# Retention and two expert layers on one core: the steps of the w_in product by quarters tied in issue order on TensorE, the softmaxes on VectorE, one more buffer for the last output weight

## Chip, cores, metric

One NeuronCore of a Trainium2 chip runs the whole program. The metric is the device time of one execution in microseconds (us). Three executions of the kernel before took 999.73 to 1002.95 us, median 1002.52. The profiled execution took 998.94 us and its span, from the first to the last instruction, is 997.2 us.

## What is computed

A decaying linear attention over 4 batches, 8 heads, 768 positions (3072 tokens of 512 values), then a gated layer (RMS norm, gate and value of 1536, silu times value, back to 512), then a second layer on which this change works:

```python
def _moe2_ref(x, w_in, w_out, g_ln):       # x: 3072 x 512
    h = x @ w_in                           # 512 -> 1024
    e = np.exp(h - np.max(h, -1, keepdims=True))
    sm = e / (np.sum(e, -1, keepdims=True) + 1e-09)
    solu = h * sm
    mu = np.mean(solu, -1, keepdims=True)
    var = np.mean((solu - mu) ** 2, -1, keepdims=True)
    ln = (solu - mu) / np.sqrt(var + 1e-06) * g_ln
    return ln @ w_out                      # 1024 -> 512
```

## The kernel before

The tokens go through in six passes of 512 (n = 0 to 5). All products are of float32 accuracy: each factor is split into a high and a low part, and a product is three matmuls, high by high, high by low, low by high. `split` (L99) does that, the high part by a cast on ScalarE (L100), the low part by a subtraction on VectorE or GpSimd (L101).

A pass has two stages. In the first (`bc_block`, in pass 5 `seven_block`, L913) the gate and value products go to the PSUM banks GB and VB (in pass 5 also SB and YB), and the output product, `cmm`, adds up over twelve weights in the banks X0 to X3; the result is the pass's x, transposed. Pieces of the next pass's attention run between (L119, banks SB and YB), with its masks on VectorE (L262).

In the second stage (`de_quarters`, L1086, in passes 2 to 5) x times w_in is made by seven products of quarter matrices in place of eight, for two blocks of 128 rows each: 14 steps, `p1` to `p7`, each of six matmuls of 128x512 in `mul` (L1136). Step names below carry the row block: p4(0) is p4 for block 0. A step's bank is emptied by a copy on ScalarE (`keep`, L1145) or by an addition on VectorE (`add`, L1149), and then serves a later step: GB takes p1(0), p6(0), p7(0), p4(0) in turn, VB takes p1(1), p6(1), p7(1), p4(1). The second operands of p5 (T1) lie in two of the four buffers "w4" in which weights are loaded; those of p6 and p7 lie in xnh and xnl, which hold the normed input of the first stage and are filled for the next pass when p6 and p7 are through: xnl by four subtractions on GpSimd, in pass 4 by three (L101).

The result has four tiles of 128 rows by 1024 columns, t = 0 to 3. `soft(t)` makes the softmax part: two maxima (L986) and their join (L987) on VectorE, two exponentials on ScalarE (L989), two products with sums on VectorE (L994), and the subtraction of the mean (L999), columns 0 to 511 on VectorE, 512 to 1023 on GpSimd. `t_tr(t)` transposes the two halves into X0 and X1 by four matmuls each (L1010) and splits each half for the output product, `e_mm(t)`: 24 matmuls into GB, X2 or X3 (L771 to L773), the first twelve with the first half. p4(0) is the last part of tile 2, p3(0) of tile 0, p4(1) of tile 3, p3(1) of tile 1, and the tiles go through in the order 2, 0, 3, 1.

No engine's order is the order of the text. A scheduler puts the instructions of each engine in order at compile time, by its own estimate of when each can start; `tc.issue_after(i)` ties the instructions of a block behind i on i's engine, and `high_priority` brings forward. Before the change the steps p1 to p7 are tied to each other hardly at all, and of the four softmaxes only soft(0) is, behind the drains that came before it.

In pass 5 the twelve output weights (512 KB each) come through two buffers "wo": `out(i)` (L919) does `cmm` for weight i and issues the load of weight i + 2, which needs the buffer that weight i has just left. Weight 11 is thus loaded once `cmm` 9 is done. The loads of xnh and xnl for the second stage (L1078) are tied behind the last of these on the SP queue.

## Time and profile before

| what | value |
|---|---|
| median of three runs (lowest, highest) | 1002.52 us (999.73, 1002.95) |
| the profiled execution's own time | 998.94 us |
| its span | 997.2 us |
| TensorE busy in the span | 966.0 us, 97% |
| VectorE, ScalarE, GpSimd busy | 506.4, 422.5, 455.6 us |
| second stage of passes 2, 3, 4, 5 begins near | 478, 640, 800, 942 us |
| last matmul begins | 993.5 us |

A group's idle time is that of its engine just before the group's instructions, and what ended it is inferred from semaphores. A matmul's time in the trace contains its run through the array: six matmuls of 128x512 in a row are issued every 0.227 us, though each shows about 0.39.

### The profile page before, as it was taken

The numbers are of one execution on the slowest core, as the hardware profiler recorded it, in microseconds if no ns is written. First come the engines' busy times: TensorE is split into PE (matmuls) and PEld (weight loads), VectorE is DVE, ScalarE is ACT, GpSimd is POOL, SyncE is SP. The second block draws the span as 40 slices with busy tenths as digits, with TensorE's granted clock in tenths as the row PEclk, the third lists the DMA queues.
The fourth block names the chain that finished last, engine by engine and source line by source line (L and its number), as shares of the span: only waits on it lengthen the run. The fifth ranks groups of instructions, "written<-read, shape, count | busy, mean of one in ns | idle before, by whom it ended". The sixth has DMA issues, their size and how long they took to land.

```text
span 997.2 us, 16099 instructions
## 1 busy us (share of the span) xinstructions
PE 966.0 (97%) x5868; PEld 800.6 (80%) x5868; DVE 506.4 (51%) x992; ACT 422.5 (42%) x824; POOL 455.6 (46%) x537
## 2 busy tenths in 40 slices
PE   8989999999999999999989999989999999999988
PEld 7867887888888888888768888868888878999866
DVE  5787784652464644333582223565223367343572
ACT  4767665581353443223463222355322356212343
POOL 6976782870242794444373244456133446000023
PEclk9899999999999999999999999999999999999999
DMA  9799999987422127997642899832699855697401
GB/s 357 248 332 400 348 314 375 344 276 233 143 64 88 49 74 248 309 307 252 228 138 94 286 333 305 298 107 99 205 332 316 312 175 170 199 313 247 170 1 43
DMA packets 94991, 227.65 MB, mean 228 GB/s; under 512 B 10816, under 2 KB 36800, under 8 KB 93888
## 3 DMA queue, kind: packets, MB, share of 16 engines
q1 hardware_dynamic: 86128, 201.44, 59.6%
q10 hardware_dynamic: 8784, 25.17, 6.5%
q8 instruction: 47, 0.77, 0.3%
q14 instruction: 32, 0.26, 0.1%
HBM read 184.63 MB, written 41.94 MB: 227 GB/s over the span
## 4 chain that ended last, share of the span: by engine, by line
PE 84%; DVE 6%; DMA 5%; ACT 2%; POOL 2%; issue 1%; SPq 0%; ACTq 0%; POOLq 0%
PE X L771 10%; PE X L773 10%; PE X L772 10%; PE GB L773 6%; PE GB L771 6%; PE GB L772 6%; PE VB L771 5%; PE VB L773 5%; PE VB L772 5%; PE SB L119 3%; PE GB L1136 2%; PE X L1136 2%; PE VB L883 2%; PE YB L883 2%; PE VB L1136 2%; DMA x<-in_wpk 2%
## 5 line engine op out<-in xcount | busy, mean ns | idle before, releaser
L790 DVE TENSOR_TENSOR f<-VB,f 128x512 f32<-128x512 f32 x60 | 41.4, 690 | 147.6 <-PE VB L773 126.0
L771 PE MATMUL X<-r,wo 128*128 128x512 f32 x264 | 102.1, 394 | 1.2 <-DMA wo<-scr 1.2
L772 PE MATMUL X<-r,wo 128*128 128x512 f32 x264 | 103.2, 391 | 0.0
L773 PE MATMUL X<-r,wo 128*128 128x512 f32 x264 | 103.0, 390 | 0.0
L819 ACT ACTIVATE f<-GB 128x512 f32<-128x512 f32 x60 | 35.8, 596 | 146.3 <-PE GB L773 143.8
L100 ACT CAST r<-f 128x512 fp32r<-128x512 f32 x72 | 44.6, 619 | 117.9 <-DVE f L790 99.5
L672 POOL TENSOR_TENSOR st<-st,x 128x512 int32<-128x512 int32 x52 | 70.0, 1349 | 47.7 <-DVE st L671 11.2
L771 PE MATMUL GB<-xnh,w 128*128 128x512 f32 (+1 forms) x220 | 85.9, 390 | 1.8 <-ACT xnh L100 1.0
L771 PE MATMUL VB<-xnh,w 128*128 128x512 f32 (+1 forms) x220 | 85.8, 390 | 0.0
L773 PE MATMUL VB<-xnh,w 128*128 128x512 f32 (+1 forms) x220 | 85.2, 387 | 0.3 <-POOL w L101 0.3
L772 PE MATMUL GB<-xnl,w 128*128 128x512 f32 (+1 forms) x220 | 85.0, 386 | 0.3 <-DVE xnl L101 0.2
L773 PE MATMUL GB<-xnh,w 128*128 128x512 f32 (+1 forms) x220 | 84.9, 386 | 0.3 <-DVE w L101 0.3
L772 PE MATMUL VB<-xnl,w 128*128 128x512 f32 (+1 forms) x220 | 85.0, 386 | 0.0
L567 POOL TENSOR_TENSOR x<-x 128x512 f32<-128x512 f32 x24 | 31.3, 1306 | 105.0 <-DMA x<-scr 66.9
L101 DVE TENSOR_TENSOR r<-f,r 128x512 fp32r<-128x512 f32 x72 | 59.8, 831 | 32.5 <-ACT r L100 31.7
L101 POOL TENSOR_TENSOR r<-st,r 128x512 fp32r<-128x512 f32 x8 | 10.3, 1293 | 115.7 <-ACT r L100 113.9
L771 PEld LDWEIGHTS X<-r,wo 128*128 128x128 f32 x264 | 49.6, 188 | 11.9 <-issue 1.6
L773 PEld LDWEIGHTS X<-r,wo 128*128 128x128 f32 x264 | 49.6, 188 | 10.4
L772 PEld LDWEIGHTS X<-r,wo 128*128 128x128 f32 x264 | 49.6, 188 | 10.1 <-issue 0.2
L771 PE MATMUL X<-w2oh,r 128*128 128x512 f32 (+1 forms) x144 | 56.7, 394 | 0.1
L773 PE MATMUL X<-w2oh,r 128*128 128x512 f32 (+1 forms) x144 | 56.4, 392 | 0.0
L772 PE MATMUL X<-w2ol,r 128*128 128x512 f32 (+1 forms) x144 | 55.7, 387 | 0.0
(445 smaller groups left out, 2474.5 us busy)
## 6 DMA issues: line engine op xcount, KB each, us to landing
w<-scr SPq DMA_DIRECT2D x96, 512.0 KB, 5.1
wo<-scr SPq DMA_DIRECT2D x60, 512.0 KB, 5.2
x<-in_wpk SPq DMA_DIRECT2D x36, 512.0 KB, 6.5
x<-scr SPq DMA_DIRECT2D x24, 512.0 KB, 6.1
sscr<-x SPq DMA_DIRECT2D x24, 512.0 KB, 7.8
scr<-CV ACTq DMA_DIRECT2D x18, 512.0 KB, 6.3
rv<-in_kv SPq DMA_DIRECT2D x24, 256.0 KB, 4.6
scr<-w ACTq DMA_DIRECT2D x12, 512.0 KB, 5.9
```

Of the source, the lines that this page charges most:

```text
L100: h = nc.scalar.copy(hi, src)
L101: (lo_eng or nc.vector).tensor_tensor(out=lo, in0=src, in1=hi.bitcast(F32), op=ALU.subtract)
L119: return lambda: nc.tensor.matmul(out, lhsT=lhsT, rhs=rhs, start=start, stop=stop)
L567: nc.gpsimd.tensor_tensor(out=w[:, 0, :], in0=w[:, 0, :], in1=w[:, 1, :], op=ALU.add)
L672: nc.gpsimd.tensor_tensor(out=ti, in0=ti, in1=lo, op=ALU.add)
L771: nc.tensor.matmul(ps, lhsT=lh, rhs=rh, start=start, stop=False)
L772: nc.tensor.matmul(ps, lhsT=lh, rhs=rl, start=False, stop=False)
L773: return nc.tensor.matmul(ps, lhsT=ll, rhs=rh, start=False, stop=stop)
L790: recent["dve"] = nc.vector.tensor_tensor(out=a, in0=GV[1], in1=silu[:, 0, :], op=ALU.mult)
L819: recent["act"] = nc.scalar.activation(s[:, 0, :], GV[0], AF.Silu)
L883: nc.tensor.matmul(ps, lhsT=x, rhs=y[:, k, :], start=start and k + i == 0, stop=k == 1 and i == 2, skip_group_check=True)
L1136: nc.tensor.matmul(bank, lhsT=x[:, k, ts_], rhs=y[:, k, :], start=start and k + i == 0, stop=k == 1 and i == 2, skip_group_check=True)
```

## The change

Four edits:

- `mul`: each of its matmuls is tied behind the one before it, so that TensorE issues the steps in the order of the text: p1(0), p1(1), p2(0), p6(0), p5(0), p7(0), p6(1), p4(0), p3(0), p7(1), p5(1), p2(1), p4(1), then the transposes of tile 2, then p3(1).
- p3(1) is tied behind the transposes of tile 2 on TensorE, and its addition behind the low parts of tile 2 on VectorE (`recent["t"]`, `recent["lo"]`, noted in `t_tr`).
- On VectorE soft(3) is tied behind the mean subtraction of soft(0) and the low parts of tile 2; soft(1) behind the mean subtraction of soft(3).
- In pass 5 weight 11 gets a buffer of the pool "x2" and its load is issued in `out(8)`.

```diff
@@ seven_block, out(i)
                 cmm(base + i, i)
-                if i + 2 < NM:
+                if i + 2 < NM - 1:
                     w_load(base + i + 2, 2)
+                if i + 3 == NM - 1:
+                    t = wsp[base + NM - 1, 2] = wt("x2", [P, 2, 512], F32R, 4)
+                    nc.sync.dma_start(t.bitcast(F32), scr[NM - 1][2])
@@ t_tr
-            run([lambda j=j: nc.tensor.transpose(bank[:, j * P:j * P + P], u[:, b, j * P:j * P + P], ident)
+            recent["t"] = run([lambda j=j: nc.tensor.transpose(bank[:, j * P:j * P + P], u[:, b, j * P:j * P + P], ident)
                  for j in range(4)])
             hi, lo = r2(), r2()
-            split(hi, lo, bank)
+            nc.scalar.copy(hi, bank)
+            recent["lo"] = nc.vector.tensor_tensor(out=lo, in0=bank, in1=hi.bitcast(F32), op=ALU.subtract)
@@ de_quarters, mul
-                    nc.tensor.matmul(bank, lhsT=x[:, k, ts_], rhs=y[:, k, :], start=start and k + i == 0,
-                                     stop=k == 1 and i == 2, skip_group_check=True)
+                    with tc.issue_after(last["mm"].ins) if "mm" in last else nullcontext():
+                        last["mm"] = nc.tensor.matmul(bank, lhsT=x[:, k, ts_], rhs=y[:, k, :],
+                                                      start=start and k + i == 0, stop=k == 1 and i == 2,
+                                                      skip_group_check=True)
@@ de_quarters, after p4(1)
-        soft(n, 3, (VB, u[3][:, 1, :]), halves(e2()), u[3], False)
-        p3(1, X3)
-        soft(n, 1, (u[1][:, 0, :], u[1][:, 1, :]), halves(e2()), u[1], True)
+        with tc.issue_after(recent["sub"].ins), tc.issue_after(recent["lo"].ins):
+            soft(n, 3, (VB, u[3][:, 1, :]), halves(e2()), u[3], False)
+        last["mm"] = recent["t"]
+        with tc.issue_after(recent["lo"].ins):
+            p3(1, X3)
+        with tc.issue_after(recent["sub"].ins):
+            soft(n, 1, (u[1][:, 0, :], u[1][:, 1, :]), halves(e2()), u[1], True)
```

The instructions are the same in number and kind; what moves is their order. On TensorE in the second stage of pass 2 (f4_572 is tile 2 after its softmax, VB takes p4(1), X3 takes p3(1)), before, right behind the end of p4(1) and 16 attention matmuls:

```order
L1010 MATMUL X0_68<-ident_182,f4_572_4605 128x128 x4
L1136 MATMUL X3_71<-w2ih_1728,r2_566_4561 128x512
L1136 MATMUL X3_71<-w2il_1729,r2_566_4561 128x512
L1136 MATMUL X3_71<-w2ih_1728,r2_567_4562 128x512
L1136 MATMUL X3_71<-w2ih_1728,r2_566_4561 128x512
L1136 MATMUL X3_71<-w2il_1729,r2_566_4561 128x512
L1136 MATMUL X3_71<-w2ih_1728,r2_567_4562 128x512
L1010 MATMUL X1_69<-ident_182,f4_572_4605 128x128 x4
```

And now, right behind p4(1):

```order
L1013 MATMUL X0_68<-ident_182,f4_572_4605 128x128 x4
L1013 MATMUL X1_69<-ident_182,f4_572_4605 128x128 x4
L1141 MATMUL X3_71<-w2ih_1728,r2_566_4561 128x512
L1141 MATMUL X3_71<-w2il_1729,r2_566_4561 128x512
L1141 MATMUL X3_71<-w2ih_1728,r2_567_4562 128x512
L1141 MATMUL X3_71<-w2ih_1728,r2_566_4561 128x512
L1141 MATMUL X3_71<-w2il_1729,r2_566_4561 128x512
L1141 MATMUL X3_71<-w2ih_1728,r2_567_4562 128x512
```

The second half's transposes come ahead of p3(1); in passes 3 and 5 they moved in the same way, and in pass 4 six matmuls of pass 5's first product stand between the two halves. Further up, p4(0) was the 11th of the steps and is now the 8th, and p5(1) was the 9th in pass 4 and is now the 11th.

On VectorE in the second stage of pass 5 (sm_1104 is tile 0, sm_1110 tile 3, sm_1112 tile 1; X0 holds the first half of tile 2's transposes), before:

```order
L986 TENSOR_REDUCE sm_1104_8868<-f4_1096_8779 128x1 x2
L986 TENSOR_REDUCE sm_1110_8918<-VB_67 128x1
L986 TENSOR_REDUCE sm_1112_8938<-f4_1097_8787 128x1
L986 TENSOR_REDUCE sm_1110_8918<-x2_1101_8851 128x1
L101 TENSOR_TENSOR r2_1106_8892<-X0_68,r2_1105_8891 128x512
L987 TENSOR_REDUCE sm_1104_8868<-sm_1104_8868 128x1
L1149 TENSOR_TENSOR f4_1097_8787<-X3_71,f4_1097_8787 128x512
```

And now:

```order
L989 TENSOR_REDUCE sm_1104_8868<-f4_1096_8779 128x1 x2
L1155 TENSOR_TENSOR f4_1097_8787<-X2_70,f4_1097_8787 128x512
L990 TENSOR_REDUCE sm_1104_8868<-sm_1104_8868 128x1
L997 SCALAR_TENSOR_TENSOR f4_1096_8779,sm_1104_8868<-f4_1096_8779,st_1102_8866 128x512
L997 SCALAR_TENSOR_TENSOR f4_1096_8779,sm_1104_8868<-f4_1096_8779,st_1103_8867 128x512
L1022 TENSOR_SCALAR sm_1104_8868<-sm_1104_8868 128x1
L1017 TENSOR_TENSOR r2_1106_8892<-X0_68,r2_1105_8891 128x512
```

Tile 0 is carried through ahead of the maxima of tiles 3 and 1, which stand behind the low parts of tile 2.

On the SP queue at the end of pass 5's first stage (wo and x2_1073 take output weights, xnh and xnl the operands of p6 and p7), before:

```order
L700 DMA wo_1059_8483<-scr8_2_113 128x1024
L872 DMA A_1060_8505<-scr11_0_120 128x2x256
L700 DMA wo_1062_8524<-scr9_2_116 128x1024
L872 DMA A_1063_8545<-scr11_1_121 128x2x256
L1082 DMA w4_1079_8702<-t2scr0_135 128x1024
L1082 DMA w4_1080_8703<-t2scr0_135 128x1024
L700 DMA wo_1072_8631<-scr10_2_119 128x1024
L700 DMA wo_1078_8700<-scr11_2_122 128x1024
L1078 DMA xnh_78<-t2scr1_136 128x2048
L1078 DMA xnl_79<-t2scr2_137 128x2048
```

And now:

```order
L925 DMA x2_1073_8633<-scr11_2_122 128x1024
L700 DMA wo_1059_8483<-scr8_2_113 128x1024
L872 DMA A_1060_8505<-scr11_0_120 128x2x256
L700 DMA wo_1062_8524<-scr9_2_116 128x1024
L872 DMA A_1063_8545<-scr11_1_121 128x2x256
L1086 DMA w4_1079_8702<-t2scr0_135 128x1024
L1086 DMA w4_1080_8703<-t2scr0_135 128x1024
L700 DMA wo_1072_8631<-scr10_2_119 128x1024
L1082 DMA xnl_79<-t2scr2_137 128x2048
L1082 DMA xnh_78<-t2scr1_136 128x2048
```

The load of weight 11 moved ahead of those of weights 8, 9 and 10, and xnl's load ahead of xnh's.

## Rows read from the trace of the kernel before

**Rows 1.** The page, part 1: busy time, share of the span, instructions.

```profile
PE 966.0 (97%) x5868; PEld 800.6 (80%) x5868; DVE 506.4 (51%) x992; ACT 422.5 (42%) x824; POOL 455.6 (46%) x537
```

**Rows 2.** By stretch: us; busy PE, PEld, DVE, ACT, POOL; PEclk, DMA share, GB/s.

```profile
540.00:640.00 100.00, 100.00 (x561) 82.20 (x560) 33.18 (x58) 27.63 (x54) 38.82 (x44) 1.00 0.89 300
...
478.00:540.00 62.00, 56.81 (x382) 45.79 (x381) 36.80 (x91) 31.67 (x67) 33.74 (x50) 1.00 0.40 131
640.00:700.00 60.00, 55.81 (x390) 44.92 (x389) 36.79 (x89) 30.78 (x65) 34.18 (x51) 1.00 0.39 123
798.00:835.00 37.00, 33.69 (x172) 27.85 (x171) 29.16 (x70) 22.69 (x49) 24.16 (x23) 1.00 0.41 141
935.00:994.00 59.00, 52.85 (x262) 42.54 (x260) 31.07 (x78) 25.01 (x54) 15.75 (x26) 1.00 0.16 61
```

**Rows 3.** TensorE's waits: us in total, times, longest us.

```profile
PE X L1010 <- DVE f L999: 4.9, 4, 1.7
PE SB L119 <- DVE A L262: 4.1, 2, 2.0
PE VB L1136 <- ACT x L1145: 2.7, 3, 0.9
PE YB L119 <- ACT sq L321: 2.5, 2, 1.2
PE GB L773 <- DVE sm L987: 1.9, 2, 1.0
...
PE X L771 <- DMA wo<-scr: 1.2, 1, 1.2
...
PE SB L883 <- POOL xnl L101: 0.9, 1, 0.9
...
PE X L1010 <- DVE r L101: 0.4, 1, 0.4
```

**Rows 4.** Timeline of TensorE, pass 5: start, us, what, [idle before <-releaser].

```profile
946.22 1.52 PE L1136 MATMUL GB<-xnh,r 128*128 128x512 f32 x6
...
958.23 0.39 PE L1136 MATMUL X<-w2ih,r 128*128 128x512 f32 x1
959.52 0.50 PE L1136 MATMUL VB<-w2ih,x 128*128 128x512 f32 x1 [0.90 <-ACT x L1145]
...
966.04 0.50 PE L773 MATMUL GB<-w2oh,r 128*128 128x512 f32 x1 [1.00 <-DVE sm L987]
...
973.01 1.26 PE L1010 MATMUL X<-ident,f 128*128 128x128 f32 x8 [1.69 <-DVE f L999]
```

**Rows 5.** Timeline of VectorE, pass 5: tile 2 from its maximum to its mean subtraction.

```profile
957.30 0.69 DVE L986 TENSOR_REDUCE sm<-GB 128x1 f32<-128x512 f32 x1 [3.36 <-PE GB L1136]
...
961.33 0.49 DVE L999 TENSOR_SCALAR f<-f,sm 128x512 f32<-128x512 f32 x1
```

**Rows 6.** Timeline of GpSimd, pass 5.

```profile
961.49 1.77 POOL L999 TENSOR_SCALAR f<-f,sm 128x512 f32<-128x512 f32 x1
```

**Rows 7.** Timeline of GpSimd, pass 2.

```profile
493.95 5.03 POOL L101 TENSOR_TENSOR xnl<-xT,xnh 128x512 fp32r<-128x512 f32 x4 [2.07 <-PE VB L1136]
...
501.68 1.57 POOL L999 TENSOR_SCALAR f<-f,sm 128x512 f32<-128x512 f32 x1
...
515.32 1.81 POOL L999 TENSOR_SCALAR f<-f,sm 128x512 f32<-128x512 f32 x1
```

**Rows 8.** Timeline of VectorE, pass 2.

```profile
515.69 1.09 DVE L994 SCALAR_TENSOR_TENSOR f<-f,x 128x512 f32<-128x512 f32 x1
```

**Rows 9.** Timeline of TensorE, pass 2.

```profile
497.05 0.39 PE L1136 MATMUL X<-w2ih,r 128*128 128x512 f32 x1
```

**Rows 10.** Timeline of TensorE, pass 4.

```profile
815.36 0.39 PE L1136 MATMUL X<-w2ih,r 128*128 128x512 f32 x1
```

**Rows 11.** Timeline of GpSimd, pass 4.

```profile
812.93 3.77 POOL L101 TENSOR_TENSOR xnl<-xT,xnh 128x512 fp32r<-128x512 f32 x3 [2.82 <-PE VB L1136]
```

**Rows 12.** DMA issues of 805 to 822 us: KB each, median us to landing.

```profile
w<-scr SPq DMA_DIRECT2D x1, 256.0 KB, 3.5
```

More of the change, by code (lines that the diff above doesn't have):

```diff
@@ L1129, in de_quarters @@
         T2, T3 = ((t[:, 0:2], t[:, 2:4]) for t in (xnh, xnl))
-        sl = [base]
+        sl, last = [base], {}
         def mul(bank, t, A, B, start=False):
@@ L1154, in de_quarters @@
         (GB, VB), (X0, X1, X2, X3) = GV, XB
-        u, last = {}, {}
+        u = {}
         def p1(t, Z):
```

## The prediction

> **What bounds the kernel now.** I read the page's first part, then the stretches, then TensorE's waits, then the timelines of the second stages. TensorE is busy 966.0 of 997.2 us [rows 1], so all that an order of issue can win is its 31 us of idle time, wherever that is not filling or draining. The stretches say where it is not: in the body of pass 3, from 540 to 640 us, TensorE has no idle time at all, while the four windows around the second stages, 218 us in all, have 5.2, 4.2, 3.3 and 6.2 us of it (62.00 less 56.81, and so on), 18.8 us together, at a granted clock of 1.00 throughout [rows 2]. The list of waits names them: eight kinds, 16 waits, 18.6 us [rows 3]. None of them is a lack of work in general. Each is one matmul at the head of TensorE's queue whose operand is late, while work for which nothing was missing stood behind it: p4(1) behind a copy of VB by ScalarE (2.7 us), transposes behind a mean subtraction (4.9 us), attention behind squares and masks that queued among four softmaxes (2.5 and 4.1 us).
>
> A wait costs a little more than its idle time. The last matmul of p3(0) was issued at 958.23 and the next, at a pace of 0.227 us (six in 1.36 us: the first of p6(0) starts at 946.22 and its six end 1.52 us later, 0.16 of it the last one's run through the array), was due at 958.46. It came at 959.52, 1.06 us late for an idle time of 0.90 [rows 4]. So 0.16 us more for each, 2.6 us for the 16: the waits cost 21.2 us. That is the ceiling of the gain.
>
> **The change part by part.** Nothing is added or removed but the place of instructions, so each part is costed by the waits that it ends and those that it makes.
>
> *Weight 11's buffer.* TensorE stood 1.2 us for this load [rows 3]. Its new place on the SP queue is ahead of the loads of weights 8 to 10, all of which landed in time before, and the buffer was last used for block 4. Gain 1.2 + 0.16 = 1.35 us, between 1.0 (if the operands for p6 become late next) and 1.35. What now follows it on the queue, xnl and xnh, is first used 4.1 us and 6.8 us into the second stage (xnh by p6(0), the 4th step, xnl by p7(0), the 6th, at 1.36 us a step) and is issued earlier than before; I take nothing for it.
>
> *Steps in order, pass 5.* p4(0) is the 8th step in place of the 11th, so tile 2's softmax begins 3 x 1.36 = 4.1 us earlier. Before, it took 4.5 us from its maximum at 957.30 to the end of the mean subtraction at 961.82 [rows 5], and GpSimd's half another 1.4 us, to 963.26 [rows 6]. Three steps back from 957.30 is 953.2, so the halves are done at 957.7 and 959.2. The 13 steps, which begin at 942.14, end at 942.14 + 13 x 1.36 = 959.8. Both transposes of tile 2 find their operand ready: that wait and the one for the copy of VB are gone, the copy now having two steps (2.7 us) between p7(1) and p4(1). Next is the output product of tile 2. Its third matmul needs the low part of the first half, and is due at 959.8 + 1.3 (eight transposes, as at 973.01) + 1.36 (p3(1)) + 0.45 = 962.9, where it came at 966.04 before [rows 4]. VectorE has seven operations of 128x512 between 957.7 and the end of that low part (two additions, two maxima, two products, the low part), at 0.69 us each [rows 5] 4.8 us, which gives 962.5; if the products must wait a us for ScalarE's exponentials, 963.5. I take a wait of 0.5 us (0 to 1.2) and so 963.4: 2.6 us gained. The later waits of the pass, 1.7 and 0.4 us with 0.16 each, 2.4 us, were those for tiles 0 and 3, whose mean subtractions now come one after the other with an output product of 5.4 us (24 x 0.227) between; I take both as gone. With the weight, pass 5 gains 6.4 us (4 to 7.2).
>
> *Passes 2 and 3.* Waits before: 0.9 for the copy, 1.2 for squares, 2.0 for masks in each (a third or a half of the totals in [rows 3]), and 1.0 for a subtraction in pass 2: 5.2 and 4.2 us of idle time [rows 2], 5.8 and 4.7 with the 0.16. What is late next is GpSimd. Its half of tile 2's subtraction stands behind the four subtractions for the next pass's xnl, which start when p7(1) has read xnl and take 5.03 us, from 493.95 to 498.98 [rows 7]. p7(1) is the 10th step before and now, so that does not move. The half then ends at 498.98 + 0.2 + 1.57 = 500.8. Before, the transposes that need it stood behind p3(1) and later waits hid it; now they come straight after the first half's. Twelve steps are done 0.227 us after 497.05 [rows 9], the thirteenth at 498.6, the first half's transposes at 499.3: a new wait of 1.5 us, 1.7 with its restart, in each of the passes, with p3(1) and all else behind it. GpSimd may be slower still: the same half took 1.81 us at 515.32, beside a VectorE product that took 1.09 in place of 0.69 [rows 7, 8]; that adds 0.25. I take 1.8 us for each. The masks and squares no longer queue among softmaxes: the attention products stand twelve output matmuls later. Gain 4.0 and 2.9 us (2 to 5.8, 1 to 4.7).
>
> [...]
>
> *Pass 4.* Waits before 3.3 us [rows 2], 3.8 with restarts. Twelve steps end at 815.58 [rows 10], the thirteenth at 816.9, the first transposes at 817.5. Six matmuls of pass 5 come next, whose weights wait for a buffer of T1, free when p5(1) is done, two steps later than before: 814.2, and 3.5 us to land [rows 12], 817.7. Then the second half's transposes: GpSimd is through xnl at 816.70 [rows 11], and 0.2 + 1.81 later at 818.7, when TensorE is there at 818.4. Two waits of 0.2 and 0.3 with restarts, 0.8 us. Gain 3.0 us (1.5 to 3.8).
>
> **Sum.** 6.4 + 4.0 + 2.9 + 3.0 = 16.3 us. Against the profiled execution's own 998.94 that is 982.6. The three runs stand 0.8 to 4.0 us above that execution, their median 3.6; in such runs I expect 983.4 to 986.6, and put down **984.8**. All upper ends (7.2 + 5.8 + 4.7 + 3.8 = 21.5, with the profiled execution's own level) give 977.4, all lower ends (8.5, at the median's level) 994.
>
> **Rivals.**
>
> *GpSimd and the chain behind it hold more.* In passes 2 to 4 the low parts of tile 2, and by the new ties soft(3), p3(1)'s addition and soft(1), stand behind transposes that stand behind GpSimd. If each half takes 1.5 us longer than I summed, as it would with one more GpSimd operation of 1.3 to 1.8 us ahead of it, the waits come again at tile 3's transposes and at the masks. For it: those spans on GpSimd are the least sure. Passes 2 to 4 then gain some 3 us of 9.9, the sum is 9.4, the time 991.7. Chance 0.15.
>
> *The passes' bodies take it back.* The transfers are busy 0.89 of the body at 540 to 640 us [rows 2]; if they set the pace there, TensorE arriving earlier only waits later for weights. Against it: TensorE waits for no weight there now, the second stages leave transfers at 0.40, and each load is set off by TensorE's own progress. Only pass 5 then gains: 998.94 - 6.4, with the runs' level 995. With pass 5 at its lower end it is inside 0.3% (some 3 us, what a measurement of this kernel can tell from no change). Chance 0.08.
>
> *Slower: the softmaxes one by one.* Before, the maxima, exponentials and products of tiles 0, 3 and 1 overlapped on VectorE and ScalarE; tied, tile 3 starts only behind tile 2's second low part, and tile 1 behind tile 3, each a chain of 4.5 us [rows 5] and GpSimd's 1.8. In pass 5 nothing else is left for TensorE. By the same count tile 3's second half is done some 1 us before its transposes are due. To lose 3 us in all, the four passes would have to lose the 16.3 us and 3 more, 4.8 us each, so each chain must run about 6 us longer than its rows: then 1004 to 1008. Against it: between the tiles TensorE has 5.4 us of output product each. Chance 0.05.
>
> *It does next to nothing*, because the scheduler had the order nearly so. Against it: p4(0) moves by three steps in all four passes. What would be left is the weight's 1.35 us. Chance 0.04.
>
> **Numbers.** The forecast has 0.68. Faster by over 0.3%: it, the first rival and most of the second, 0.89; within 0.3%: 0.06; slower: 0.05. The range for 8 in 10 takes in the forecast's own span and the first rival's time: 978 to 994.
>
> **What would show it.** Right: no wait for the weight near 938 us; no wait of VB's p4(1) on ScalarE; about 1.5 us of wait at the second transposes in passes 2 and 3, ended by GpSimd's subtraction and none such in pass 5; TensorE's idle time in the four windows down from 18.8 to some 5 us; the bodies without waits. Wrong: a wait of over 3 us at any transposes, waits for weights in a body, or waits at tile 3's or tile 1's transposes in pass 5.

## The result, and the profile after

| | before | after |
|---|---|---|
| median of the runs | 1002.38 us (four, 999.73 to 1002.95) | 989.88 us (four, 989.03 to 991.99) |
| ratio, with 95% interval | | 0.9884 (0.986 to 0.9908) |
| the profiled execution, its span | 998.94, 997.2 us | 989.03, 987.2 us |

A second set on another occasion gave 990.05 us against 1003.2, ratio 0.988 (0.9854 to 0.9905). The change makes the kernel 1.2% faster, 12.5 us between the medians. Faster was forecast, and the time lies within the range, but 5 us above the forecast of 984.8 and nearer to the first rival's 991.7.

From one start of p1(0) to the next in TensorE's timeline, and from the last to the last matmul, the profiled executions compare as follows. This leaves out the start of the program up to pass 2's second stage, which no edit touches and which took 478.6 to 484.5 us in the executions profiled for this study. The kernel before's profiled execution is one of its faster ones (998.94 us at a granted clock of 0.997; 43 others took 998.06 to 1006.67 at 0.988 to 0.995), which may be why the table gives 10.4 us and the medians 12.5.

| stretch, us | before | after | difference | forecast |
|---|---|---|---|---|
| pass 2's second stage, pass 3's first | 160.83 | 158.85 | -1.98 | -4.0 |
| pass 3's second stage, pass 4's first | 159.79 | 158.20 | -1.59 | -2.9 |
| pass 4's second stage, pass 5's first | 142.89 | 141.30 | -1.59 | -3.0 - 1.35 |
| pass 5's second stage | 51.38 | 46.14 | -5.24 | -5.05 |
| sum | 514.89 | 504.49 | -10.40 | -16.3 |

Pass 5 came as summed. Passes 2 to 4 gave 3.7 us of 9.9, the weight's part left out.

In the rows of after, t_tr's and soft's lines stand 3 further than before and `mul` at L1141: L997 is soft's product, L999 the join of its sums, L1002 the mean subtraction, L1013 the transposes, L1017 the low part, L1151 `keep`, L1155 `add`. The page's part 1 (as [rows 1]):

```profile
PE 966.5 (98%) x5868; PEld 803.6 (81%) x5868; DVE 511.7 (52%) x992; ACT 422.0 (43%) x824; POOL 455.3 (46%) x537
```

By stretch (columns as in [rows 2]), a body first, then the four second stages:

```profile
540.00:636.00 96.00, 96.00 (x543) 78.92 (x542) 31.83 (x55) 24.45 (x47) 39.47 (x45) 1.00 0.90 305
478.00:540.00 62.00, 59.87 (x391) 48.70 (x390) 39.83 (x89) 33.10 (x71) 32.75 (x49) 0.97 0.40 135
637.00:697.00 60.00, 56.84 (x369) 46.23 (x367) 37.30 (x87) 32.01 (x69) 34.36 (x51) 1.00 0.41 133
796.00:833.00 37.00, 34.07 (x171) 27.76 (x170) 30.42 (x70) 21.74 (x46) 22.88 (x21) 1.00 0.37 129
930.00:984.00 54.00, 53.03 (x270) 44.03 (x268) 32.44 (x81) 26.53 (x57) 14.49 (x26) 1.00 0.13 53
```

The body has no idle time, as before, so the transfers took nothing back. The second stages still have 2.1, 3.2, 2.9 and 1.0 us, 9.2 where 18.8 were and 5 forecast, and in the first the granted clock is 0.97. TensorE's waits (as [rows 3]):

```profile
PE X L1013 <- POOL f L1002: 4.8, 3, 2.1
PE GB L773 <- DVE r L1017: 2.0, 2, 1.7
...
PE X L1141 <- DVE r L101: 1.1, 2, 0.5
...
PE SB L119 <- DVE A L262: 0.9, 1, 0.9
```

Of the eight kinds before, six are gone, those for VB's copy, the squares, the weight and VectorE's mean subtraction among them; of the masks one of two is left. The third matmul of tile 2's output product still waits for the low part, 1.71 us in pass 4 and 0.26 in pass 5. Before, it waited 0.88 and 1.00 there, under the name of the join L987 in [rows 3, 4]: the low part ended at 965.98 us, 0.06 ahead of the matmul, and the join in the same moment as the matmul began. What is new: the second transposes wait for GpSimd's half of tile 2 (2.13, 2.12 and 0.54 us in passes 2, 3 and 4, none in pass 5), and p5(0) for S1's low part (0.54 in passes 4 and 5). Pass 2 in the timelines, GpSimd first, then VectorE (between its rows the mean of tile 2 is made), then TensorE:

```profile
494.37 5.67 POOL L101 TENSOR_TENSOR xnl<-xT,xnh 128x512 fp32r<-128x512 f32 x4 [1.62 <-PE VB L1141]
500.00 0.19 POOL L1024 TENSOR_TENSOR sm<-sm 128x1 f32<-128x1 f32 x1
500.17 1.57 POOL L1002 TENSOR_SCALAR f<-f,sm 128x512 f32<-128x512 f32 x1
```

```profile
494.43 0.68 DVE L997 SCALAR_TENSOR_TENSOR f<-GB,x 128x512 f32<-128x512 f32 x1
...
495.03 1.18 DVE L997 SCALAR_TENSOR_TENSOR f<-f,x 128x512 f32<-128x512 f32 x1
...
496.27 1.11 DVE L999 TENSOR_TENSOR sm<-sm 128x1 f32<-128x1 f32 x1
...
497.61 1.29 DVE L1002 TENSOR_SCALAR f<-f,sm 128x512 f32<-128x512 f32 x1
498.82 0.68 DVE L1155 TENSOR_TENSOR x<-X,x 128x512 f32<-128x512 f32 x1
```

```profile
499.06 0.60 PE L1013 MATMUL X<-ident,f 128*128 128x128 f32 x4
501.79 0.65 PE L1013 MATMUL X<-ident,f 128*128 128x128 f32 x4 [2.13 <-POOL f L1002]
```

The four subtractions for xnl took 5.67 us where they had taken 5.03 [rows 7]. Beside them three VectorE operations were drawn out: a product of two SBUF tiles 1.18 us, an addition of two columns 1.11, a mean subtraction 1.29. In pass 5, with no GpSimd operation on two tiles beside them, the same three take 0.69, 0.15 and 0.49. Operations that read PSUM (the product from GB, the addition from X) kept 0.68, and so did the maxima. The softmax of tile 2, three steps earlier than before, has moved onto the subtractions, and each holds up the other. In pass 4 GpSimd's quarter subtractions for pass 5 (L437) meet tile 0's products in the same way:

```profile
816.79 2.98 POOL L437 TENSOR_TENSOR xT<-xT 128x512 f32<-128x512 f32 x2
```

```profile
817.36 1.27 DVE L997 SCALAR_TENSOR_TENSOR f<-f,st 128x512 f32<-128x512 f32 x1 [0.94 <-ACT st L992]
...
818.56 1.76 DVE L997 SCALAR_TENSOR_TENSOR f<-f,st 128x512 f32<-128x512 f32 x1
...
820.38 0.67 DVE L1017 TENSOR_TENSOR r<-X,r 128x512 fp32r<-128x512 f32 x1
```

```profile
821.11 0.49 PE L773 MATMUL GB<-w2oh,r 128*128 128x512 f32 x1 [1.71 <-DVE r L1017]
```

And behind the wait of 2.13 us TensorE ran at half clock for a while (0.51 granted, in the first of these windows), as it did not behind that of 2.12 us in pass 3 (windows, columns as above):

```profile
502.70:506.10 3.40, 3.40 (x9) 2.61 (x9) 3.36 (x11) 3.33 (x10) 1.43 (x3) 0.51 0.00 0
661.50:664.90 3.40, 3.27 (x15) 2.37 (x14) 3.35 (x11) 3.33 (x10) 1.40 (x3) 1.00 0.00 0
```

At 0.51 the matmuls come every 0.427 us in place of 0.227; eight of them cost 1.6 us.

### The profile page after: what moved, and what is told of

It reads as the page before. It is cut to its first block, busy times and chain, and to the rows that moved or that the text cites. A ratio compares the mean times of both kernels' runs of the same rounds, so it can differ in the third digit from the quotient of the medians.

```text
span 987.2 us, 16094 instructions
## 1 busy us (share of the span) xinstructions
PE 966.5 (98%) x5868; PEld 803.6 (81%) x5868; DVE 511.7 (52%) x992; ACT 422.0 (43%) x824; POOL 455.3 (46%) x537
## 4 chain that ended last, share of the span: by engine, by line
PE 85%; DVE 5%; POOL 3%; DMA 2%; ACT 2%; issue 1%; SPq 0%; ACTq 0%; POOLq 0%; DVEq 0%
PE X L771 11%; PE X L772 10%; PE X L773 10%; PE GB L773 6%; PE GB L771 6%; PE GB L772 6%; PE VB L771 6%; PE VB L772 5%; PE VB L773 5%; PE SB L119 3%; PE YB L119 2%; PE VB L883 2%; PE YB L883 2%; PE GB L1141 2%; PE X L1141 2%; PE X L1013 2%
## 5 line engine op out<-in xcount | busy, mean ns | idle before, releaser
L772 PE MATMUL X<-r,wo 128*128 128x512 f32 x260 | 101.9, 392 | 0.0
L773 PE MATMUL X<-r,wo 128*128 128x512 f32 x260 | 101.4, 390 | 0.0
L771 PE MATMUL X<-r,wo 128*128 128x512 f32 x260 | 99.7, 394 | 0.0
L773 PEld LDWEIGHTS X<-r,wo 128*128 128x128 f32 x260 | 48.8, 188 | 10.2
L771 PEld LDWEIGHTS X<-r,wo 128*128 128x128 f32 x260 | 48.8, 188 | 10.2 <-ACT r L100 0.2
L772 PEld LDWEIGHTS X<-r,wo 128*128 128x128 f32 x260 | 48.8, 188 | 10.0 <-issue 0.2
```

The lines of the kernel that those rows point to most:

```text
L771: nc.tensor.matmul(ps, lhsT=lh, rhs=rh, start=start, stop=False)
L772: nc.tensor.matmul(ps, lhsT=lh, rhs=rl, start=False, stop=False)
L773: return nc.tensor.matmul(ps, lhsT=ll, rhs=rh, start=False, stop=stop)
```

## Experiments

Two theories of what was missing in passes 2 to 4. **Exclusion**: VectorE's products of SBUF tiles, additions and mean subtractions, with all operands in SBUF, and a running GpSimd operation hold each other up (in pass 2 a product of 0.69 us took 1.18, the four subtractions 5.67 for 5.03), and the change put such pairs side by side. **Queue**: GpSimd's half is late by its place in GpSimd's queue alone, the low part by its place in VectorE's, and the long durations have another cause. All runs below are told by the four stretches of the table above and their sum (after: 504.49).

**All of xnl behind tile 2's half.** `recent["g2"]` is GpSimd's subtraction in soft(2); in pass 4 the second and third of three are tied in the same way.

```diff
-    def xn_split_t(k):
-        with tc.issue_after(recent["hi"].ins):
+    def xn_split_t(k, n):
+        with tc.issue_after(recent["hi"].ins), tc.issue_after(recent["g2"].ins) if n > 2 and k >= 0 else nullcontext():
             split(xnh[:, k, :], xnl[:, k, :], xT[:, k, :], nc.gpsimd)
...
```

> The changed kernel with the subtractions for the next pass's xnl (four in passes 2 and 3, the second and third in pass 4) tied on GpSimd behind tile 2's half of the mean subtraction. Theory of exclusion (a VectorE operation whose operands all lie in SBUF and a running GpSimd operation hold each other up): with nothing on GpSimd beside it, tile 2's softmax in pass 2 goes back to 0.69 us for the second product (1.18 in the changed kernel), 0.15 for the join of the sums (1.11) and 0.49 for the mean subtraction (1.29); GpSimd's half ends near 498.2 and not at 501.74; the waits of 2.13 and 2.12 us at the second transposes are gone, and TensorE's stretch at half clock after 502.7 with the first of them. But the four subtractions now run beside tile 0's two products, which take 1.2 us or more each, and tile 2's low part behind them comes 0.5 to 1.7 us late at the third matmul of tile 2's output product. Passes 2 and 3 together gain 2 to 5 us against the changed kernel. Theory of the queue alone (GpSimd's half is late because it stands fifth in its queue, and VectorE's long operations have another cause): the three operations stay at 1.18, 1.11 and 1.29 us, the half begins right after them near 498.9 and ends near 500.5 with a wait of 0.8 us left, tile 0's products stay at 0.69 us, and no new wait comes: 3.5 to 5 us gained.

Measured: 156.92, 157.03, 140.19 and 46.15 us, sum 500.29; ratio to the kernel before 0.9843 (0.9827 to 0.986). VectorE in pass 2, tile 2's softmax and then tile 0's products, and TensorE:

```profile
498.25 0.69 DVE L997 SCALAR_TENSOR_TENSOR f<-f,x 128x512 f32<-128x512 f32 x1
...
498.99 0.15 DVE L999 TENSOR_TENSOR sm<-sm 128x1 f32<-128x1 f32 x1
...
499.36 0.49 DVE L1002 TENSOR_SCALAR f<-f,sm 128x512 f32<-128x512 f32 x1
...
503.31 1.04 DVE L997 SCALAR_TENSOR_TENSOR f<-f,st 128x512 f32<-128x512 f32 x1 [0.94 <-ACT st L992]
...
504.27 1.77 DVE L997 SCALAR_TENSOR_TENSOR f<-f,st 128x512 f32<-128x512 f32 x1
...
506.10 0.68 DVE L1017 TENSOR_TENSOR r<-X,r 128x512 fp32r<-128x512 f32 x1
```

```profile
501.26 5.91 POOL L101 TENSOR_TENSOR xnl<-xT,xnh 128x512 fp32r<-128x512 f32 x4
```

```profile
506.83 0.50 PE L773 MATMUL GB<-w2oh,r 128*128 128x512 f32 x1 [1.59 <-DVE r L1017]
```

The three operations are back at 0.69, 0.15 and 0.49 us, the two waits of 2.1 us are gone, and the lengthening went with the subtractions to tile 0's products (1.04 and 1.77 us). The three durations are to the hundredth what the theory of exclusion gave. The queue alone would have left the durations and made no new wait. Gain 4.2 us over the change, 1.6 of it the half clock that the change's execution had in pass 2.

The other traces say the same, and set a limit to it. In the fourteen profiled executions, from 478 us on, 158 VectorE operations on SBUF alone (products, additions, low parts, mean subtractions) began inside a GpSimd operation on two tiles of 128x512, at least 0.1 us after its start and 0.7 before its end. None of them ended before it did. The 199 products of two SBUF tiles that had no GpSimd operation of 128x512 beside them took 0.67 to 0.69 us. Beside GpSimd's mean subtraction, which reads one tile, it is otherwise: all 37 that began inside it in this way ended inside it, the products after 0.68 to 1.09 us.

**The quarter subtractions of pass 4 behind tile 0's half** (`recent["g0"]`, on GpSimd).

```diff
-            return lambda: nc.gpsimd.tensor_tensor(out=out, in0=a, in1=b, op=ALU.subtract)
+            def f():
+                with tc.issue_after(recent["g0"].ins):
+                    nc.gpsimd.tensor_tensor(out=out, in0=a, in1=b, op=ALU.subtract)
+            return f
```

> The changed kernel with the four subtractions of quarter matrices for pass 5's first product (in pass 4, on GpSimd) tied behind GpSimd's half of tile 0's mean subtraction. Theory of exclusion: in pass 4 tile 0's two products, 1.27 and 1.76 us beside two of those subtractions, take 0.69 us each; tile 2's low part ends near 819.5 and not at 821.05; the wait of 1.71 us at the third matmul of tile 2's output product falls to 0.3 or less; pass 4 gains 1.4 to 1.9 us, unless the operands that now come up to 4 us later are waited for before pass 5's first products (up to 2 us lost near 828 to 838). Theory of the queue alone: the two products keep 1.27 and 1.76 us or so, the wait stays at 1.5 us or more, and nothing is gained.

Measured: 158.85, 158.21, 144.13 and 46.25 us, sum 507.44. Tile 0's products, then tile 3's second product and mean subtraction, on VectorE (this file's lines are 3 further; L993 is the join of the maxima), and TensorE:

```profile
817.07 0.69 DVE L1000 SCALAR_TENSOR_TENSOR f<-f,st 128x512 f32<-128x512 f32 x1 [0.94 <-ACT st L995]
...
817.77 0.69 DVE L1000 SCALAR_TENSOR_TENSOR f<-f,st 128x512 f32<-128x512 f32 x1
...
824.05 1.08 DVE L1000 SCALAR_TENSOR_TENSOR x<-x,x 128x512 f32<-128x512 f32 x1
...
825.56 1.53 DVE L1005 TENSOR_SCALAR x<-x,sm 128x512 f32<-128x512 f32 x1
...
828.20 0.68 DVE L1020 TENSOR_TENSOR r<-X,r 128x512 fp32r<-128x512 f32 x1
```

```profile
819.26 0.50 PE L776 MATMUL GB<-w2oh,r 128*128 128x512 f32 x1 [0.18 <-DVE r L1020]
828.94 0.66 PE L1016 MATMUL X<-ident,x 128*128 128x128 f32 x4 [2.43 <-DVE sm L993]
```

The products fell to 0.69 us each and the wait from 1.71 to 0.18, as by exclusion. But the subtractions, and what is made from them on GpSimd, now meet tile 3's softmax, whose product and mean subtraction take 1.08 and 1.53 us (0.69 and 1.27 in the changed kernel). Behind them on VectorE stands tile 0's low part (828.20 in the last row), and tile 3's transposes, which need its bank, start 0.06 us after its end with 2.43 us of wait (the join that the profile names ends in the same moment). Half clock follows (matmuls every 0.43 us from 830.72 to 833.71), and pass 4 is 2.8 us worse. The drawing out accounts for 0.65 of the 2.43 us. The rest goes with another shift: in the changed kernel 22 matmuls of pass 5's first product stand ahead of tile 3's transposes (828.09 to 830.76 us), and these need what the moved subtractions make; here they are issued from 844.45 us on, and nothing fills the wait. No run parts the two.

**Two of xnl behind, two ahead**: as the first run, with `k >= 2` in the condition.

> The changed kernel with only the last two of the four subtractions for the next pass's xnl tied behind GpSimd's half of tile 2 (passes 2 and 3; in pass 4 the second and third, as in the run with all four). Theory of exclusion: tile 2's second product and the join of its sums still stand beside the first two subtractions (1.18 and 1.11 us), the mean subtraction does not (0.49 and not 1.29); GpSimd's half runs from about 497.6 to 499.2 on the changed kernel's scale, before its transposes are due at 499.66: no wait there. The two that follow end near 501.9, before tile 0's products begin at 502.2, which therefore take 0.69 us, and tile 2's low part is at most 0.3 us late. Both waits gone: passes 2 and 3 last some 155.2 to 155.6 us each from one second stage to the next, 1.4 us less than with all four tied (156.92 and 157.03). Rival (the low part's wait of 1.59 us in that run came from the order of VectorE's queue and not from GpSimd beside it): the wait stays at 1.3 us or more and the two stretches at 156.5 to 157.

Measured: 157.69, 158.83, 141.79 and 46.26 us, sum 504.57. A miss. Tile 2's second product (1.41 us) and the join (1.11) stood beside the two early subtractions, so all of VectorE behind them came some 1.7 us later than in the first run (the mean subtraction 18.78 us after p1(0), against 17.09), tile 0's exponentials on ScalarE too, and tile 2's high part stands behind those: TensorE waited 0.97 us for it, a wait that neither theory had, then 0.64 for the low part. Half clock in passes 3 and 4 took some 3.2 us of the 4.3 by which the sum lies above the first run's. By the runs' times the two versions can't be told apart (ratio 0.9862, 0.9831 to 0.9892, against 0.9843).

**The parts of the change alone.** The weight's buffer alone:

> The kernel before with the new buffer for output weight 11 alone. If the buffer is worth what was summed: TensorE's wait of 1.18 us at 937.8 is gone, the stretch from pass 4's end to the first matmul of pass 5's second stage is 1.3 us shorter than before, everything earlier stays in place, and the time is 1.3 us (0.13%) below the kernel before. Rival: the loads behind it become late in its place (xnh and xnl for p6 and p7), a new wait of 0.5 to 1.3 us by a DMA appears in pass 5's second stage, and the gain is 0 to 0.8 us.

Measured: ratio 0.9983 (0.9971 to 0.9996). The third stretch is 141.47 us, 1.42 less than before, and no wait for p6 or p7 appeared; the other three are as before but for 1.5 us of half clock in pass 3 (0.72 granted over 672 to 678 us). So the 1.35 us stand.

The ties on TensorE with the weight, without those on VectorE:

> The changed kernel without its three ties on VectorE (soft(3), soft(1) and p3(1)'s addition are free again); TensorE's ties and the weight stay. If TensorE's order carries the gain: the waits of p4(1) for ScalarE's copy stay away, tile 2's second transposes still wait some 2.1 us for GpSimd in passes 2 and 3, and the time is within 1.5 us of the changed kernel's 989.9. If VectorE's ties are as much of it: the maxima of tiles 3 and 1 come ahead of tile 0's products again, the waits for masks and for tile 0's and 3's mean subtractions return at 1 to 2 us each, three or more of them in passes 2 to 5, and the time is 993 to 997 us.

Measured: 159.36, 159.45, 141.15 and 48.48 us, sum 508.44; ratio 0.9904 (0.9886 to 0.9921). Between the two: the waits for VB's copy are gone and the masks' with them. The expected wait of 2.1 us at the second transposes doesn't show, since TensorE now takes two matmuls of the output product ahead of them: in passes 2 and 3 it waits 2.6 us there for the high part of tile 2, with half clock behind it, and in pass 5 1.15 us for a mean subtraction.

The ties on VectorE alone, with TensorE's order and the weight as before:

> The kernel before with the ties on VectorE alone (soft(3) behind tile 0's mean subtraction and tile 2's low parts, soft(1) behind tile 3's, p3(1)'s addition behind tile 2's low parts); TensorE's order and the weight's buffer as before. If the ties on VectorE need TensorE's order: TensorE's four waits for VB's copy (0.9 us each) stay, tile 3's and 1's maxima now stand behind low parts that come as late as before, and the time is within 2 us of the kernel before, or up to 3 us above it. If they carry a part of their own: the waits for squares and masks in passes 2 and 3 (1.2 and 2.0 us each) fall by half or more, pass 5's waits of 1.0 and 1.7 us go, and the time is 3 to 6 us below.

Measured: 157.94, 158.40, 143.33 and 49.21 us, sum 508.88; ratio 0.9945 (0.9918 to 0.9973). The copy's waits of 0.9 us stay and, against the expectation, the squares' 1.25; the masks' waits fall from 2.0 to 0.29 us, pass 5's 1.0 and 1.7 go (one of 0.9 for a high part comes). In these executions the ties on VectorE bring 6.0 us by themselves, those on TensorE 5.0 (514.89 - 508.44 - 1.42), the weight 1.4, and all together 10.4. But the run with TensorE's ties lost some 3.2 us to half clock in two passes, the changed kernel 1.6 in one, and the run with VectorE's ties none in its second stages. By the ratios TensorE's ties with the weight are 0.8 to 1.1% below the kernel before and VectorE's 0.3 to 0.8%. Either alone gives a good part of the gain; which carries more is not shown.

**The order of the steps**: p6(1) and p7(0) ahead of p5(0).

```diff
         p6(0, GB)
+        p6(1, VB)
+        p7(0, GB, f4())
         p5(0, X1)
-        p7(0, GB, f4())
         c22(0, X1)
-        p6(1, VB)
         p4(0, GB)
```

> The changed kernel with the steps in the order p6(0), p6(1), p7(0), p5(0), p4(0) in place of p6(0), p5(0), p7(0), p6(1), p4(0). If p5(0)'s wait of 0.54 us (0.70 with the restart) in passes 4 and 5 is only the low part of S1 being due too early: it is gone in both, p7(0) finds GB copied (one step of 1.36 us between), and passes 4 and 5 are 0.7 us shorter each. Rival: tile 2's second half is then complete one step before p4(0) and not three; its maximum comes in VectorE's way of the first half's, the softmax of tile 2 starts up to 0.4 us later, GpSimd's half with it, and passes 2 and 3 lose 0.2 to 0.5 us each.

Measured: 158.39, 158.41, 141.61 and 45.40 us, sum 503.81. p5(0)'s wait is gone in both passes; pass 5 gains 0.74. In pass 4 xnh is wanted before its load is in (0.28 us), p4(0) waits 0.34 for ScalarE's copy, and nothing is gained. The half clock, with the same two waits of 2.13 and 2.12 us, is in pass 3 this time and not in pass 2.

Both together, the last two of xnl late and this order:

> Both: the last two subtractions for xnl behind GpSimd's half of tile 2, and p5(0) behind p7(0). If the two parts add: passes 2 and 3 at 155.2 to 155.8 us each, pass 4 with pass 5's first stage at 139.5 (140.19 with the subtractions alone, less 0.7), pass 5's second stage at 45.4: in all 6.5 us below the changed kernel. If the later maximum of tile 2 eats the room that the two subtractions leave, a wait of 0.3 to 0.6 us comes back at the second transposes or the low part of tile 2: 5 to 5.5 us below.

Measured: 159.33, 157.34, 139.97 and 45.34 us, sum 501.98; the waits of 0.98 and 0.64 us of the run with two late are in passes 2 and 3, with half clock in pass 2. Pass 5 is as expected, pass 4 half a us above (p4(0) waits 0.34 for ScalarE's copy). In all that is 2.5 us below the change where 6.5, or 5 to 5.5, was expected: a miss, by the same wait for tile 2's high part as in the run with two late.

The same with the second to fourth quarter subtraction behind tile 0's half:

> As the run before, and in pass 4 the second to fourth subtraction of quarter matrices behind GpSimd's half of tile 0 (the first stays ahead of it). By exclusion only one of tile 0's two products then stands beside a subtraction (1.3 us in place of two at 1.27 and 1.76): the wait of some 1.4 us at the third matmul of tile 2's output product falls to 0.5 or less. Against it the three operations behind the half run beside tile 3's softmax, as in the run with all four behind it, where tile 3's transposes waited 2.43 us: if so, that wait returns with 1 us or more and pass 4 gains nothing or loses up to 1.5 us against the run before.

Measured: 157.75, 159.60, 141.61 and 45.33 us, sum 504.29. The low part's wait in pass 4 stays at 1.66 us: here the last subtraction for xnl and the first quarter subtraction are beside tile 0's products (1.10 and 1.76 us). A miss: the wait did not fall to 0.5 us, because other GpSimd work took the place of what was moved, and no wait came at tile 3's transposes either. Half clock is in passes 3 and 4.

**Tile 2's high and low part first.** Since a GpSimd operation must stand beside something, let it be something that nothing soon waits for. `mid` is tile 2's first high and low part; all of xnl behind tile 2's half; the new order of steps.

```diff
-            nc.scalar.activation(e[hf], H[hf], AF.Exp, bias=nmx, accum_out=se[:, hf:hf + 1])
+            with behind(0):
+                nc.scalar.activation(e[hf], H[hf], AF.Exp, bias=nmx, accum_out=se[:, hf:hf + 1])
...
-            V.scalar_tensor_tensor(out=u[:, hf, :], in0=H[hf], scalar=1.0, in1=e[hf],
-                                   op0=ALU.mult, op1=ALU.mult, accum_out=su[:, hf:hf + 1])
+            with behind(1):
+                V.scalar_tensor_tensor(out=u[:, hf, :], in0=H[hf], scalar=1.0, in1=e[hf],
+                                       op0=ALU.mult, op1=ALU.mult, accum_out=su[:, hf:hf + 1])
...
-        with tc.issue_after(last["act"].ins), tc.issue_after(last["dve"].ins):
-            soft(n, 0, (u[0][:, 0, :], u[0][:, 1, :]), (st(), st()), u[0], False)
+        drained = last["act"], last["dve"]
         p2(1, X2)
         t_tr(2, (X0, X1))
+        with tc.issue_after(drained[0].ins), tc.issue_after(drained[1].ins):
+            soft(n, 0, (u[0][:, 0, :], u[0][:, 1, :]), (st(), st()), u[0], False, recent["mid"])
         p4(1, VB)
```

(`behind(i)` is `tc.issue_after(mid[i].ins)` where `mid` is given.)

> A version meant to beat the changed kernel: all subtractions for the next pass's xnl behind GpSimd's half of tile 2 (as in the first run of these), p5(0) behind p7(0), and tile 2's first high and low part ahead of tile 0's exponentials (on ScalarE) and products (on VectorE), with tile 0's maxima left where they were. By the theory of exclusion tile 0's products, held up to 1.8 us by the subtractions, no longer stand ahead of the low part: the wait of 1.59 us at the third matmul of tile 2's output product (passes 2 and 3, 1.42 in pass 4, 0.25 in pass 5) is gone, and tile 0's transposes come some 4 us later than that, so that they are not waited for either. Passes 2 and 3 at 155.0 to 155.7 us each, pass 4 with pass 5's first stage at 138.3 to 139, pass 5's second stage at 44.9 to 45.3: 9 to 10.5 us below the changed kernel, near 980. Rival: the lateness only moves on (tile 0's softmax begins 0.9 us later, is drawn out by the subtractions, and the second low part of tile 2, tile 0's transposes or the masks wait 1 to 2 us in each of passes 2 to 4): 985 to 987, as in the run with the subtractions alone.

Measured: 155.81, 155.99, 141.04 and 45.75 us, sum 498.59; ratio 0.9833 (0.9812 to 0.9855). Passes 2 and 3 are 0.1 and 0.3 us above what the theory gave, with a wait of 0.4 us left in each. In pass 4 the lateness moved on, as the rival had it: 1.44 us for tile 3's first product, which frees VB for pass 5's, and 0.51 for a low part; pass 5 loses 0.50 to a high part. In all that is 5.9 us below the change and not 9 to 10.5, and the median of 985.10 us is in the rival's range: the version comes near its numbers in passes 2 and 3 alone.

**Each where it paid**: that in passes 2 and 3, the earlier arrangement in passes 4 and 5.

> The version of before this run, with tile 2's high and low part ahead of tile 0's exponentials and products in passes 2 and 3 alone; passes 4 and 5 as in the run with the step order and two subtractions late. Stretches seen apart should add: 155.8 and 156.0 us for passes 2 and 3, 140.0 for pass 4 with pass 5's first stage, 45.3 for pass 5's second stage, 397.1 in all against 404.5 of the changed kernel: 7.4 us less, and as much less in the medians of this call to within 1.5 us. If what pass 4 had gained depends on how pass 3 leaves the queues of ScalarE and GpSimd, pass 4 stays at 141 us, and the gain is 6.4 us. A stretch of TensorE at half clock behind a wait adds 1 to 2 us to any stretch in which it falls.

> The changed kernel unaltered, on the same chip as the run before it: stretches of 157.3 (158.9 if TensorE falls to half clock behind the wait of 2.1 us) and 156.6 to 158.3 us, 141.3 and 46.1 us; its waits of 2.1 us in passes 2 and 3 and of 1.7 us in pass 4 in the same places. If the half clock belongs to a place in the program, it is again in pass 2 and not in pass 3; if it only follows some of the long waits, it can be in either, both or neither.

(Both sums in the first text are 100 short: 497.1 and 504.5 are meant.) Measured: 155.79, 155.91, 140.02 and 45.33 us, sum 497.05, each within 0.1 us of its expectation; median 981.87 us, ratio to the kernel before 0.9803 (0.9776 to 0.983). The changed kernel on the same chip: 158.86, 158.21, 141.33 and 46.26 us, sum 504.66, median 990.05. This version is 8.2 us below the change and 21.3 below the kernel before. Its waits in the second stages:

```profile
PE GB L773 <- DVE r L1022: 1.7, 2, 1.5
...
PE X L1018 <- DVE f L1007: 0.8, 2, 0.4
...
PE GB L1148 <- ACT f L1158: 0.3, 1, 0.3
...
PE SB L883 <- DMA w<-scr: 0.2, 1, 0.2
```

Its products of tile 0 in pass 2 still take 1.30 and 1.78 us beside xnl. Behind them TensorE still waits 0.4 us in each of passes 2 and 3, for tile 0's mean subtraction (the second row).

## Why the prediction held, and where its sum was too high

- **Weight 11's buffer, 1.35 us.** Right: 1.42 alone, and nothing behind it on the queue became late.
- **Pass 5, 5.05 us without the weight.** Right in its waits, and right in amount (5.24) partly by luck, since two errors cancel. The third matmul of tile 2's output product comes 21.74 us after p1(0) and came 23.90 after it before: 2.2 us gained where 2.6 was summed. It waits 0.26 us where 0.5 was taken, but p5(0)'s 0.54 was not in the sum: p5(0) now comes ahead of p6(1), a step earlier than before, and asks for S1's low part. That takes 1.37 us beside GpSimd's low part of S3, where its twin for S2 takes 0.69, another case of exclusion (so it was before the change, at 947.26 us, where nobody waited):

```profile
942.59 1.37 DVE L101 TENSOR_TENSOR r<-st,r 128x512 fp32r<-128x512 f32 x1 [0.22 <-ACT r L100]
```

```profile
942.12 1.29 POOL L101 TENSOR_TENSOR r<-st,r 128x512 fp32r<-128x512 f32 x1 [96.26 <-ACT r L100]
```

  From that third matmul to the last the pass takes 24.40 us, 27.48 before: 3.1 us gained where 2.4 was summed, since the two waits there (1.69 and 0.41) cost more than their idle time and 0.16 each.
- **Passes 2 and 3, 4.0 and 2.9 us.** The step "The half then ends at 498.98 + 0.2 + 1.57 = 500.8" failed in its first number. It named the right wait, at the right transposes, and took 5.03 us for the four subtractions from a place in the trace where no such VectorE operation stood beside them. The same change moves tile 2's softmax three steps earlier, onto them: 5.67 us, and a wait of 2.13 where 1.5 was summed. With its restart and the allowance that was taken as 1.8 (1.7 and 0.25 make 1.95), and 2.35 was measured. The first run of the experiments shows the cause, not only the time. The trace of the kernel before held the sign, in pass 4, where tile 2's second product and the join of its sums stood beside two quarter subtractions and took 1.29 and 1.09 us:

```profile
817.34 1.29 DVE L994 SCALAR_TENSOR_TENSOR f<-f,x 128x512 f32<-128x512 f32 x1 [0.26 <-ACT x L989]
...
818.68 1.09 DVE L996 TENSOR_TENSOR sm<-sm 128x1 f32<-128x1 f32 x1
```

```profile
816.78 2.98 POOL L437 TENSOR_TENSOR xT<-xT 128x512 f32<-128x512 f32 x2
```

  On top came 1.6 us of half clock in pass 2, which the sum had no term for, since [rows 2] show 1.00 throughout; and in pass 3 0.9 us for one set of masks and 0.1 for the low part.
- **Pass 4, 3.0 us.** Got 1.59 less the weight's 1.42, so 0.2. The two waits that were summed came at 0.14 and 0.54 us, where 0.2 and 0.3 were taken. The third was missed: the low part of tile 2 behind tile 0's products was worked out for pass 5 alone, and in pass 4 these take 1.27 and 1.76 us and TensorE waits 1.71, twice the 0.88 that the sum had counted as gone. p5(0)'s 0.54 is the fourth.
- **The allowance of 0.25 us.** It came from one pair of rows: GpSimd's mean subtraction took 1.81 us in place of 1.57, and the VectorE product beside it took 1.09 and ended 0.35 us before it [rows 7, 8]. Where GpSimd subtracts a mean, on one tile, the runs agree with that: all 37 VectorE operations counted above ended inside it, the products after 0.68 to 1.09 us. Where GpSimd works on two tiles they don't: none of the 158 ended before the GpSimd operation beside it, a 128x1 addition of 0.15 us took 1.11, and the subtractions for xnl were held in turn (5.67 us for 5.03). The 0.25 was not needed, since the half itself took 1.57 us in passes 2 and 3, as it did at 501.68 us in [rows 7]. What cost is that the prediction asked what GpSimd and VectorE do to each other only for the half that was seen late, and not for every pair that the change would newly set side by side.
- **The rivals.** The first, passes 2 to 4 gaining 3 us of 9.9, is the nearer in amount (3.7 us in all: 1.98 + 1.59 + 1.59 - 1.42), though not by its mechanism: GpSimd's half was 0.6 us later than summed and not 1.5. The transfers took nothing: the body is at 96.00 of 96.00 us. Softmaxes one by one made no wait at tile 3's or tile 1's transposes; the ties on VectorE alone bring 6.0 us, which had been credited mainly to TensorE's order.
- **The signs.** No wait for the weight, none of p4(1) on ScalarE, none at pass 5's second transposes, bodies without waits: as written. The waits at the second transposes in passes 2 and 3 are there, ended by GpSimd, at 2.1 us and not 1.5. Idle time in the four windows 9.2 us and not 5.

## What to carry to other kernels

When a change of order moves a chain, list what runs beside it at its new time, and ask of each pair on VectorE and GpSimd what the two took where a trace shows them together: here the products of two SBUF tiles, 0.69 us by themselves, took 1.04 to 1.78 beside GpSimd's work on two tiles, so that tile 2's 0.69 from the old trace did not hold beside its new neighbour (1.18). What paid in passes 2 and 3 was not to make the pair shorter but to put beside GpSimd's long work the VectorE work whose result is due last, and to carry what is due next past it first; in pass 4 the same order only moved the wait. And ties on either engine alone gave some 5 and 6 us against a scheduler that had placed both freely, 10.4 with both and the weight: try parts apart before crediting one of them, and look for half clock in each execution before comparing them.

## What the runs showed of the hardware

- Beside GpSimd's subtractions even the addition of two columns was drawn out, 1.11 us for 0.15, in passes 2, 3 and 4 of the changed kernel alike. VectorE operations with a PSUM input, and maxima over SBUF, kept 0.67 to 0.69 us beside the same subtractions. GpSimd's mean subtraction, on one tile, did not hold VectorE up in this way: 23 mean subtractions that began inside it took 0.48 to 0.92 us and ended inside it, where beside GpSimd's operations on two tiles 23 took 1.22 to 1.45.
- Half clock behind a wait was not fixed to a place. In the profiled executions of this study TensorE waited over 2 us 15 times in the second stages and fell to half clock for a while (0.51 granted, matmuls every 0.427 us from 502.7 to 506.1 us in the changed kernel) within 1.5 us of the end of 8 of these waits; of 16 waits of 1.4 to 1.75 us, 2 had it, and 3 of 6 pairs of waits of some 0.98 and 0.64 us close behind each other. The same wait (2.12 to 2.13 us, same transposes) had it in pass 2 and not in pass 3 in the changed kernel, twice, and the other way round with the steps reordered. In the changed kernel's pass 2 it cost some 1.6 us (eight matmuls by 0.2). What decides it stays open; no run was made for it alone.
